# Entry 0's first 512 tokens two to a partition, in four rounds of four heads: what it does to the opening of a fused retention and MLP kernel

## The chip, the core and the metric

The kernel runs on one core of one Trainium2 chip. A core has a matrix engine (PE, with its weight loads shown apart as PEld), a vector engine (DVE), an activation engine (ACT), a general engine (POOL), a queue engine (SP) and 16 DMA engines. Work on PE reads SBUF and writes PSUM, which has eight banks; DVE and ACT bring results from PSUM to SBUF. The metric is the device time of one execution in microseconds, as the median of several runs.

## What is computed

```python
q, k, v: (8, 8, 576, 64)          # entries, heads, tokens, head size
scores = q @ k^T / 8              # within an entry and a head
gamma  = 1 - 2 ** (-5 - head)
ret    = (scores * gamma ** (i - j) for j <= i, else 0) @ v
x      = ret.transpose(0, 2, 1, 3).reshape(4608, 512)
h      = x @ w_in                 # 512 -> 2048
out    = (h / (1 + exp(-1.702 * h))) @ w_out      # 2048 -> 512
```

The kernel factors `gamma ** (i - j)` into a factor of the query's position (`gq`, applied to the output), one of the key's position (`vfac`, with the 1/8 in it, applied to the values or, for one block, elsewhere), and a mask of zeros and ones.

## The kernel before

**An order written out by hand.** The program records operations engine by engine in the order in which they are called (`R.op`), and each engine executes its own list strictly in that order. Waits follow from the named tiles (`r`, `w`) and PSUM banks (`ps`); PE doesn't wait for itself, except where `own=` names one of its earlier operations.

**The retention of one entry.** Entry 0 is handled in blocks of 128 tokens (four, and one of 64 tokens). For a block, PE turns queries and keys (`transposes`, L411, eight matmuls with the identity), ACT copies them to SBUF (`evac_t`, L418), PE forms the scores of the eight heads (`scores`, L431), DVE multiplies them by the mask into `sm` (`mask_s`, L441), PE multiplies by the values (`values`: L454), adds the part that comes from earlier blocks through the running state (L482), and extends the state with this block's keys and values (L467). ACT copies the state (`evac_z`, L505), and DVE multiplies the output by `gq` into `xT` (`evac_o`, L518), the transposed input of the MLP. In the block at 384 the factor `vfac` sits in the mask (`mask3`), so that its values can be used as they come; a scaled copy (`v3`) is made afterwards for the state. Blocks of the other entries are of 64 tokens and are handled in bursts (`burst`, `step`), which are mixed into the MLP.

**Loads.** Keys, queries and values of entry 0 are loaded by POOL, which casts them from f32 to bf16 on the way: one DMA for a block's eight heads, in pieces of one head's row of one token (`load`, L219). The first queries and values come by SP without a cast (`load_early`, L265). The weights follow in POOL's list (`load_w_in` L243, `load_w_out` L248), and two multiplications of values by `vfac` stand in it (`scale_v`, L390). Later loads wait on DVE's zeroing of unused halves (`constants_third`, `constants_shifted`).

**The MLP.** `hidden(c, f)` forms 128 of the 2048 hidden columns for 512 tokens (L732, four matmuls of 512 columns; ACT applies the activation, L737); `project` multiplies by `w_out` (L765). Chunk 0 is the first 512 tokens, so it needs all four blocks. Its first four hidden units are split by tokens (`hidden_part`, L843: 384 tokens, then 128) and put between the operations of the last block; `hidden(0, 4)` is the first ordinary unit. From there on PE runs hidden units, projections and bursts to the end. `fill` (L831) is matmuls on zeros whose result isn't used.

## Time and profile before

| | |
|---|---|
| runs | 299.64 us median (298.96, 299.64, 299.91) |
| the profiled execution | 298.93 us, span 297.1 us |
| PE | 291.1 us busy (98%), 3399 matmuls |
| DVE, ACT, POOL | 123.1, 125.9, 151.6 us busy |
| `project`, L765 | 544 matmuls, 122.0 us |
| `hidden`, L732 | 492 matmuls, 108.9 us |
| granted TensorE clock | 1.000 |

The span runs from the first to the last instruction; the time of an execution has some 1.8 us more around it. Times in the views below are microseconds from the span's start. A row of the timeline gives start, duration, engine, line, operation, tile written and tiles read, the part of the array that is used (rows*columns), the shape, the count, and in brackets the idle time before it with what ended it. A matmul's duration includes its way through the array, so that the rows of one engine overlap. In the chain of waits a row is start, duration, engine, tile, line and count.

### The profile page before, as it was taken

The numbers are of one execution on the slowest core, as the hardware profiler recorded it, in microseconds if no ns is written. First come the engines' busy times: TensorE is split into PE (matmuls) and PEld (weight loads), VectorE is DVE, ScalarE is ACT, GpSimd is POOL, SyncE is SP. The second block draws the span as 40 slices with busy tenths as digits, with TensorE's granted clock in tenths as the row PEclk, the third lists the DMA queues.
The fourth block names the chain that finished last, engine by engine and source line by source line (L and its number), as shares of the span: only waits on it lengthen the run. The fifth ranks groups of instructions, "written<-read, shape, count | busy, mean of one in ns | idle before, by whom it ended". The sixth has DMA issues, their size and how long they took to land.

```text
span 297.1 us, 7697 instructions
## 1 busy us (share of the span) xinstructions
PE 291.1 (98%) x3399; PEld 148.5 (50%) x3399; DVE 123.1 (41%) x221; ACT 125.9 (42%) x208; POOL 151.6 (51%) x205
## 2 busy tenths in 40 slices
PE   7799999999999999999999999999999999999996
PEld 3464455848544444544454445545454445444444
DVE  7769475454445435532615324245326504000012
ACT  6658426617256313540355045503660275026600
POOL 8975979989959887568984797000000000000000
PEclk9999999999999999999999999999999999999999
DMA  9999999999999999999999999904820200030012
GB/s 133 156 186 190 173 171 165 188 131 140 182 140 143 183 143 175 194 130 134 154 218 124 114 188 162 85 2 108 170 38 2 107 37 2 0 108 35 0 50 93
DMA packets 154850, 36.04 MB, mean 121 GB/s; under 512 B 145472, under 2 KB 150336, under 8 KB 154816
## 3 DMA queue, kind: packets, MB, share of 16 engines
q0 software_dynamic: 116304, 18.10, 94.1%
q1 hardware_dynamic: 38512, 17.44, 32.6%
q8 instruction: 27, 0.44, 0.6%
q14 instruction: 7, 0.06, 0.1%
HBM read 36.70 MB, written 9.44 MB: 155 GB/s over the span
## 4 chain that ended last, share of the span: by engine, by line
PE 94%; POOL 2%; DMA 2%; issue 0%; DVE 0%; POOLq 0%
PE psB L765 40%; PE psB L732 36%; PE psB L749 5%; PE psA L627 2%; DMA st_k<-in_k_dram 2%; PE psA L599 2%; PE psA L641 2%; PE psA L615 1%; PE psA L765 1%; PE psA L791 1%; PE psB L843 1%; PE psA L411 1%; POOL st_k L219 1%; POOL st_q L219 1%; POOL st_v L219 1%
## 5 line engine op out<-in xcount | busy, mean ns | idle before, releaser
L765 PE MATMUL psB<-w_out_sb,gT 128*128 128x512 bf16 x544 | 122.0, 380 | 0.0
L732 PE MATMUL psB<-xT,w_in_sb 128*128 128x512 bf16 x492 | 108.9, 379 | 0.0
L737 ACT ACTIVATE gT<-psB 128x512 bf16<-128x512 f32 x123 | 73.5, 597 | 38.4 <-PE psB L732 38.1
L765 PEld LDWEIGHTS psB<-w_out_sb,gT 128*128 128x128 bf16 x544 | 51.8, 98 | 60.2 <-DVE sm L696 0.3
L732 PEld LDWEIGHTS psB<-xT,w_in_sb 128*128 128x128 bf16 x492 | 47.5, 98 | 56.5
L685 DVE TENSOR_TENSOR xT<-psA,gq 128x768 bf16<-128x768 f32 x21 | 20.1, 958 | 115.3 <-PE psA L615 115.3
L232 POOL DMA_DIRECT2D st_k<-in_k_dram x70 | 52.5, 774 | 15.2 <-DMA st_k<-in_k_dram 10.9
L774 ACT ACTIVATE osb<-psB 128x512 f32<-128x512 f32 x31 | 18.5, 597 | 90.2 <-PE psB L765 86.8
L232 POOL DMA_DIRECT2D st_v<-in_v_dram x70 | 51.9, 767 | 5.7 <-DMA st_v<-in_v_dram 3.3
L219 POOL DMA_DIRECT2D st_q<-in_q_dram x39 | 34.8, 891 | 10.2 <-DMA st_q<-in_q_dram 7.6
L390 DVE TENSOR_TENSOR st_v<-st_v,vfac 128x512 bf16<-128x512 bf16 x36 | 23.3, 681 | 1.2 <-DMA st_v<-in_v_dram 1.2
L714 DVE TENSOR_TENSOR zacc<-zacc,psA 128x256 f32<-128x256 f32 x49 | 20.5, 419 | 6.9 <-PE psA L627 5.7
L696 DVE TENSOR_TENSOR sm<-psA,maskw 128x768 bf16<-128x768 f32 x21 | 19.9, 948 | 0.0
L749 PE MATMUL psB<-xT,w_in_sb 128*128 128x256 bf16 x128 | 15.0, 273 | 0.0
L777 DVE COPY osb<-psB 128x512 f32<-128x512 f32 x3 | 2.1, 692 | 29.7 <-PE psB L765 29.7
L749 PEld LDWEIGHTS psB<-xT,w_in_sb 128*128 128x128 bf16 x128 | 12.2, 98 | 1.7
L418 ACT ACTIVATE qk<-psA 128x1024 bf16<-128x1024 bf16 x8 | 8.2, 1022 | 9.8 <-PE psA L411 9.8
L599 PE MATMUL psA<-sm,st_v 64*64 64x64 bf16 x504 | 11.8, 195 | 0.3
L627 PE MATMUL psA<-st_v,st_k 64*64 64x64 bf16 x448 | 11.8, 199 | 0.0
L627 PEld LDWEIGHTS psA<-st_v,st_k 64*64 64x64 bf16 x448 | 7.5, 105 | 8.3 <-issue 7.8
L755 ACT ACTIVATE gT<-psB 128x512 bf16<-128x512 f32 x16 | 9.4, 599 | 5.0 <-PE psB L749 5.0
L615 PE MATMUL psA<-qk,zw 64*64 64x64 bf16 x448 | 11.1, 194 | 0.0
(103 smaller groups left out, 164.3 us busy)
## 6 DMA issues: line engine op xcount, KB each, us to landing
out_dram<-osb SPq DMA_DIRECT2D x35, 256.0 KB, 3.9
st_q<-in_q_dram POOLq DMA_DIRECT2D x31, 128.0 KB, 7.5
st_k<-in_k_dram POOLq DMA_DIRECT2D x57, 64.0 KB, 7.3
st_v<-in_v_dram POOLq DMA_DIRECT2D x57, 64.0 KB, 7.0
w_out_sb<-in_moe_w_out_dram POOLq DMA_DIRECT2D x4, 512.0 KB, 10.9
w_in_sb<-in_moe_w_in_dram POOLq DMA_DIRECT2D x3, 512.0 KB, 8.6
st_k<-in_k_dram POOLq DMA_DIRECT2D x4, 128.0 KB, 4.8
w_in_sb<-in_moe_w_in_dram POOLq DMA_DIRECT2D x2, 256.0 KB, 6.8
```

The source lines that it names most:

```text
L219: paced(R.op("POOL", lambda e, d=d, s=s: e.dma_start(d, s), w=[(nm, sl, c)], dma=(nm, sl, c), own=pace()))
L232: paced(R.op("POOL", lambda e: [e.dma_start(d, s) for d, s in parts], w=[(nm, sl, c)], dma=(nm, sl, c), parts=2, own=pace()))
L390: R.op(eng, lambda e: e.tensor_tensor(t, t, f, ALU.mult), r=[("vfac", min(b, 1))], w=[("v", sl, c)])
L627: i = e.matmul(psA[half(j), bank, off + 64 * t : off + 64 * t + 64], rows_of(st_k, m_in, g, u, h), rows_of(st_v, m_in, g, u, h), start=(t ...
L685: R.op("DVE", lambda e: e.tensor_tensor(xT[:, :, t0 : t0 + 192].rearrange("p (u j) n -> p u j n", u=2), psA[:, 2:4, 0:384].rearrange("p u ...
L696: R.op("DVE", lambda e: e.tensor_tensor(o, i, k, ALU.mult), r=["maskw"], w=[("sm", si(m))], ps=["S"])
L714: R.op("DVE", lambda e, to=to, src=src, was=was: e.tensor_tensor(to, was, src, ALU.add), r=[("zacc", (blk - 1) % 3)], w=[("zacc", blk)], p ...
L732: i = e.matmul(bank, w_in_sb[:, a, 128 * f : 128 * f + 128], xT[:, a, 512 * c : 512 * c + 512], start=(a == 0), stop=(a == 3))
L737: R.op("ACT", lambda e: e.activation(gT[c % 2][:, f, :], bank, AF.Gelu_apprx_sigmoid), w=[("gT", c % 2, f)], ps=[key])
L749: m = e.matmul(bank[:, 256 * i : 256 * i + 256], w_in_sb[:, a, 128 * (f + i) : 128 * (f + i) + 128], xT[:, a, a0 : a0 + 256], start=(a == ...
L765: i = e.matmul(bank, gT[c % 2][:, f, 128 * r : 128 * r + 128], w_out_sb[:, f, :], start=(f == 0), stop=(f == NF - 1))
L774: R.op("ACT", lambda e: e.activation(osb[m].ap(), bank, AF.Copy), w=[("osb", m)], ps=[key])
```

## The change

The first 512 tokens of entry 0 are now four rounds `n = 2 G + u`: `G` is the 256 tokens from `256 G`, `u` the four heads from `4 u`. Two neighbouring tokens lie in one partition, so a piece of a load is two rows of a head (`two_rows`), and a load has 4 heads x 128 pieces; the queries of rounds 2 and 3 come in one. Positions, factors and masks get a form for even and odd tokens. Within a round, tokens are treated as two blocks of 128 (`r`), held in the two halves of the partitions: scores and values use quarters of the array (64 rows by 64 columns), the state is extended after each block (`state_two`) and read by the next, and the matmuls of `values_two` are three groups, each of which waits for the one before it (`own=done`). Round 3 has `vfac` in its mask, as the block at 384 had, and now its keys are scaled into `k3` for the state, on POOL, where `v3` was a copy of the values. `scale_two(1)` is on DVE; rounds 2 and 3 have theirs on POOL behind the weights' first DMAs. The calls of the opening are put in a new order, the first four hidden units are split by 256 tokens and by heads, the zeroing of unused halves (`constants_third(0, 1)`) now stands behind all of them, and the last two extensions of the state follow unit 7, as one did before.

```diff
+        def load_two(n, nm, count=1):
+
+            src, dst = {"q": (q, st_q), "k": (k, st_k), "v": (v, st_v)}[nm]
+            s = two_rows(src, n, count)
+            d = dst[:, 0, n : n + count, :].rearrange("p c n -> p (c n)")
+            d = d.rearrange("p (h x) -> p h x", x=2 * DH)
+            paced(R.op("POOL", lambda e: e.dma_start(d, s),
+                       w=[(nm, 0, n + i) for i in range(count)], dma=(nm, 0, n), own=pace()))
+
+        def two_rows(src, n, count=1):
+            G, u = divmod(n, 2)
+            s = src[0, 4 * u : 4 * u + 4 * count, 256 * G : 256 * G + 256, :]
+            return s.rearrange("h (p s) d -> p h (s d)", s=2)
...
+            scale_two(0)
             for r in range(2):
                 rows = slice(64 * r, 64 * r + 64)
                 R.op("DVE", lambda e, rows=rows, r=r: e.tensor_single_scalar(
                     maskw[rows, :], rel[rows, 0:64], float(-64 * r), ALU.is_ge),
                     r=["rel"], w=["maskw"])
+                R.op("DVE", lambda e, rows=rows, r=r: e.tensor_single_scalar(
+                    mask[rows, 1, 0, :], rel[rows, 0:64], float(1 - 64 * r), ALU.is_ge),
+                    r=["rel"], w=["mask"])
+            R.op("DVE", lambda e: e.tensor_copy(
+                mask[:, 0, :, :], maskw.ap().unsqueeze(1).to_broadcast([P, 2, 64])),
+                r=["maskw"], w=["mask"])
+            R.op("DVE", lambda e: e.tensor_copy(mask[:, 1, 1, :], maskw.ap()),
+                 r=["maskw"], w=["mask"])
...
+        def scale_k3(eng):
+            f = vfac[0][:, 4:8, NC + 2 : NC + 4].unsqueeze(3).to_broadcast([P, 4, 2, DH])
+            o = k3.rearrange("p (h s d) -> p h s d", s=2, d=DH)
+            R.op(eng, lambda e: e.tensor_tensor(o, two(st_k, 3), f, ALU.mult),
+                 r=[("vfac", 0), ("k", 0, 3)], w=[k3_key])
+
+        def two(t, n):
+            return t[:, 0, n, :].rearrange("p (h s d) -> p h s d", s=2, d=DH)
+
+        def scale_two(n, eng="DVE"):
+            G, u = divmod(n, 2)
+            t = two(st_v, n)
+            i = early(1).rearrange("p (h s d) -> p h s d", s=2, d=DH) if n == 0 else t
+            f = vfac[0][:, 4 * u : 4 * u + 4, NC + 2 * G : NC + 2 * G + 2]
+            f = f.unsqueeze(3).to_broadcast([P, 4, 2, DH])
+            R.op(eng, lambda e: e.tensor_tensor(t, i, f, ALU.mult),
+                 r=[("vfac", 0)] + (early_keys(1) if n == 0 else []), w=[("v", 0, n)])
+
+        def transposes_two(n, at=None):
+            to, key = turned(at)
+
+            def fn(e):
+                for a, t in ((0, st_q), (1, st_k)):
+                    for s2 in range(2):
+                        for h in range(4):
+                            i = e.matmul(to[half(h % 2), a, 2 * s2 + h // 2, :],
+                                         two(t, n)[:, h, s2, :], ident.ap(),
+                                         is_transpose=True)
+                return i
+            R.op("PE", fn, r=["ident", ("q", 0, n), ("k", 0, n)], ps=[key])
+
+        def intra_two(n, pair):
+            at, keys = pairs[pair]
+            now = qk[n]
+
+            def fn(e):
+                for hp in range(2):
+                    for s2 in range(2):
+                        for r in range(2):
+                            for j in range(2):
+                                o = at[half(r), j, 2 * hp + s2, :]
+                                i = e.matmul(o.rearrange("p (s n) -> p s n", s=2),
+                                             now[half(j), 1, 2 * s2 + hp, half(r)],
+                                             now[half(j), 0, hp : 4 : 2, half(r)])
+                return i
+            R.op("PE", fn, r=[("qk", n, 0), ("qk", n, 1)], ps=keys)
+            m = mask.ap().rearrange("p k s n -> p (k s n)").unsqueeze(1).to_broadcast([P, 4, 256])
+            if n == 3:
+                m = mask3.rearrange("p (x y) -> p x y", y=256)
+            o = sm_all[n % 3].ap().rearrange("p (x y) -> p x y", y=256)
+            i = at.rearrange("p a (h k) n -> p (a h) (k n)", k=2)
+            R.op("DVE", lambda e: e.tensor_tensor(o, i, m, ALU.mult),
+                 r=mask3_keys if n == 3 else ["mask"], w=[("sm", n % 3)], ps=keys)
+
+        def state_two(n, r, out=True):
+            u = n % 2
+            ks = k3.rearrange("p (h s d) -> p h s d", s=2, d=DH) if n == 3 else two(st_k, n)
+
+            def fn(e):
+                for hp in range(2):
+                    for s2 in range(2):
+                        for j in range(2):
+                            h = 2 * hp + j
+                            i = e.matmul(psZ[half(j), 2 * u + hp, 0:64],
+                                         ks[half(r), h, s2, :],
+                                         two(st_v, n)[half(r), h, s2, :],
+                                         start=(n == 0 and r == 0 and hp == 0 and s2 == 0),
+                                         stop=False, skip_group_check=True)
+                return i
+            R.op("PE", fn, r=[k3_key if n == 3 else ("k", 0, n), ("v", 0, n)], ps=["Z"])
+            if out:
+                R.op("ACT", lambda e: e.activation(
+                    zq[r][:, 2 * u : 2 * u + 2, :], psZ[:, 2 * u : 2 * u + 2, 0:64], AF.Copy),
+                    w=[("zq", r, u)], ps=["Z"])
+
+        def values_two(n, o, inter_first=True):
+            po, key = o
+            G, u = divmod(n, 2)
+
+            def inter(e):
+                for r in range(2):
+                    if G == 0 and r == 0:
+                        continue
+                    for hp in range(2):
+                        for j in range(2):
+                            i = e.matmul(po[half(j), 2 * hp : 2 * hp + 2, half(r)],
+                                         zq[1 - r][half(j), 2 * u + hp, :],
+                                         qk[n][half(j), 0, hp : 4 : 2, half(r)],
+                                         start=(inter_first and hp == 0 and r == (G == 0)),
+                                         stop=not inter_first,
+                                         skip_group_check=True)
+                return i
+
+            def rows(e, r):
+                for hp in range(2):
+                    for s2 in range(2):
+                        for j in range(2):
+                            x = sm[n % 3][half(r), j, 2 * hp + s2, :]
+                            i = e.matmul(po[half(j), 2 * hp : 2 * hp + 2, half(r)],
+                                         two(st_v, n)[half(r), 2 * hp + j, s2, :],
+                                         x.rearrange("p (s n) -> p s n", s=2),
+                                         start=(not inter_first and r == hp == s2 == 0),
+                                         stop=(inter_first and s2 == 1), skip_group_check=True)
+                return i
+            parts = [(lambda e, r=r: rows(e, r), [("sm", n % 3), ("v", 0, n)]) for r in range(2)]
+            zs_of = [("zq", r, u) for r in range(1 + G)]
+            parts.insert(0 if inter_first else 2, (inter, [("qk", n, 0)] + zs_of))
+            done = None
+            for fn, reads in parts:
+                done = R.op("PE", fn, r=reads, ps=[key], own=done)
+            t0 = 256 * G
+            to = xT[:, 2 * u : 2 * u + 2, t0 : t0 + 256].rearrange("p h (n s) -> p h s n", s=2)
+            by = gq[:, 2 * u : 2 * u + 2, t0 : t0 + 256].rearrange("p h (n s) -> p h s n", s=2)
+            R.op("DVE", lambda e: e.tensor_tensor(
+                to, po.rearrange("p (h s) n -> p h s n", s=2), by, ALU.mult),
+                r=[("gq", 0), ("gq", 1)],
+                w=[("xU" if u else "xT", x) for x in range(4 * G, 4 * G + 4)], ps=[key])
...
-        load(0, 0, "k")
+        load_two(0, "k")
         constants_first()
-        load(0, 1, "qk")
-        load(0, 2, "qk")
-        load(0, 1, "v")
-        load(0, 2, "v")
-        load(0, 3, "qk")
+        load_two(1, "q")
+        load_two(1, "k")
+        load_two(1, "v")
+        load_two(2, "q", 2)
+        load_two(2, "k")
+        load_two(2, "v")
+        load_two(3, "k")
         load_w_in(0, 1)
+        load_two(3, "v")
         load_w_in(1, 2)
-        scale_v(1, "POOL")
-        scale_v(2, "POOL")
-        load(0, 3, "v")
         load_w_in(2, 4)
+        scale_two(2, "POOL")
+        scale_k3("POOL")
...
+        split = [(psW, "W"), (psU, "U"), (psA[:, 0, :], "S"), (psA[:, 2, :], "O")]
+        fourth = (psH[0].rearrange("p (h n) -> p h n", h=HP), ("H", 0))
+
+        def hidden_part(f, lo, hi, us=(0, 1)):
             bank, key = split[f]
 
             def fn(e):
-                for a in range(4):
-                    i = e.matmul(bank[:, lo:hi], w_in_sb[:, a, 128 * f : 128 * f + 128],
-                                 xT[:, a, lo:hi], start=(a == 0), stop=(a == 3))
-                return i
-            R.op("PE", fn, r=[("w_in", f // 2)] + [("xT", x) for x in range(lo // 64, hi // 64)],
-                 ps=[key])
-            if hi == 512:
+                for u in us:
+                    for a in (2 * u, 2 * u + 1):
+                        i = e.matmul(bank[:, lo:hi], w_in_sb[:, a, 128 * f : 128 * f + 128],
+                                     xT[:, a, lo:hi], start=(a == 0), stop=(a == 3),
+                                     skip_group_check=True)
+                return i
+            R.op("PE", fn, r=[("w_in", f // 2)] + [("xU" if u else "xT", x) for u in us
+                                                   for x in range(lo // 64, hi // 64)], ps=[key])
+            if hi == 512 and 1 in us:
                 R.op("ACT", lambda e: e.activation(gT[0][:, f, :], bank, AF.Gelu_apprx_sigmoid),
                      w=[("gT", 0, f)], ps=[key])
...
         fill(11)
         later_gq(0)
+        transposes_two(0)
+        evac_t(0)
+        state_two(0, 0)
         later_gq(1)
-        transposes(0)
-        evac_t(0)
+        fill(3)
+        intra_two(0, 0)
+        transposes_two(1, second)
+        evac_t(1, second)
+        state_two(0, 1)
+        scale_two(1)
         later_gq(2)
+        fill(2)
+        intra_two(1, 1)
+        values_two(0, third[0])
+        state_two(1, 0)
+        later_gq(3)
+        fill(2)
+        values_two(1, third[1])
+        state_two(1, 1)
+        transposes_two(2)
+        evac_t(2)
         constants_mask3()
-        fill(4)
-        transposes(1, second)
-        evac_t(1, second)
-        intra(0)
-        fill(4)
-        intra(1, 1)
-        transposes(2)
-        evac_t(2)
-        values(0, third[0])
-        evac_z(0)
-        evac_o(0, third[0])
-        later_gq(3)
-        fill(2, second)
-        intra(2)
-        values(1, third[1])
-        evac_z(1)
-        evac_o(1, third[1])
-        fill(1)
-        transposes(3)
+        fill(2)
+        intra_two(2, 0)
+        state_two(2, 0)
+        transposes_two(3)
         evac_t(3)
-        values(2, third[0])
-        evac_z(2)
-        evac_o(2, third[0])
-        fill(1)
         gelu_table()
-        intra(3)
+        hidden_part(1, 0, 256)
+        intra_two(3, 1)
+        values_two(2, third[0])
+        hidden_part(0, 0, 256)
+        state_two(3, 0)
+        hidden_part(2, 0, 256)
+        values_two(3, fourth, False)
+        for f in range(3):
+            hidden_part(f, 256, 512, (0,))
+        hidden_part(3, 0, 256)
+        hidden_part(3, 256, 512, (0,))
+        for f in range(4):
+            hidden_part(f, 256, 512, (1,))
         constants_third(0, 1)
...
-        hidden(0, 4, (psA[:, 0, :], "S"))
-        for f in range(5, NF):
+        hidden(0, 4, wide_banks[2])
+        hidden(0, 5, wide_banks[1])
+        for f in range(6, NF):
             hidden(0, f, next_bank())
             if f == 7:
-                values(3, third[0], "state")
-                evac_z(3)
+                state_two(2, 1, False)
+                state_two(3, 1, False)
+                evac_z()
```

## What I predict

> **What bounds the kernel now.** I read the page's slices first, then the busy time by stretches, then the chain in order of time, then the waits, and last single PE rows.
>
> ```profile
> PE   7799999999999999999999999999999999999996
> PEclk9999999999999999999999999999999999999999
> ...
> 10.00:20.00 10.00, 8.48 (x138) 5.38 (x138) 6.76 (x11) 5.07 (x8) 8.84 (x12) 1.00 1.74 169
> 20.00:30.00 10.00, 9.97 (x66) 4.89 (x65) 9.33 (x22) 7.32 (x15) 6.67 (x9) 1.00 1.21 193
> ```
>
> The first number after each stretch's length is PE's busy time: 8.48 of 10 us up to 20 us, 9.97 afterwards. From about 21 us PE never waits again, so whatever happens later on another engine is hidden as long as that stays so, and the change is worth exactly what it moves the start of the first ordinary hidden unit (`hidden(0, 4)`, whose weight load starts at 21.57), plus matmuls added or removed after it.
>
> ```profile
> 8.74 6.04 DMA st_k<-in_k_dram
> 14.91 0.61 PE psA L411 x8
> 15.52 0.34 PE psA L454 x8
> 15.99 0.36 PE psA L482 x8
> 16.37 0.70 DVE xT L518
> 17.12 2.12 PE psB L843 x12
> ...
> PE psA L411 <- DMA st_k<-in_k_dram: 1.3, 1, 1.3
> ```
>
> The chain says that the opening is set by the issue of ten loads on POOL and the landing of the last keys at 14.78 (issue 8.74, 6.0 to landing); PE waited 1.3 us for them. From there to 21.57 are 6.7 us, nearly all PE work. So an earlier landing is worth something only if PE, ACT and DVE have finished the earlier rounds by then, and if the 6.7 us stay 6.7.
>
> **Prices of PE work**, from these rows:
>
> ```profile
> 14.91 0.38 PE L411 MATMUL psA<-ident,st_q 128*128 128x128 bf16 x4 [1.32 <-DMA st_k<-in_k_dram]
> 15.13 0.39 PE L411 MATMUL psA<-ident,st_k 128*128 128x128 bf16 x4
> 15.45 0.41 PE L454 MATMUL psA<-sm,st_v 128*64 128x128 bf16 x8
> 15.70 0.29 PE L467 MATMUL psA<-st_v,st_k 128*64 128x64 bf16 x8
> 15.92 0.41 PE L482 MATMUL psA<-qk,zq 64*64 64x128 bf16 x8
> 16.26 0.39 PE L831 MATMUL psB<-idle 128*128 128x512 bf16 x1
> ...
> 65.22 0.27 PE L615 MATMUL psA<-qk,zw 64*64 64x64 bf16 x12
> 65.57 0.26 PE L599 MATMUL psA<-sm,st_v 64*64 64x64 bf16 x8
> ```
>
> - One matmul of 128 columns runs 0.22, of which it holds the array 54 ns (four whole-array ones in 0.38). Eight that alternate between two halves take 0.41, so 27 ns each; 64 columns, half. Groups over all four quadrants: L641 has 24 of 64 columns in 0.40, (0.40 - 0.20) / 23 = 9 ns each; for 128 columns I take 54 / 4 = 13.5.
> - Tail: the next engine starts 0.18 + 0.05 after the last slot of a group.
> - Change of array shape: the state group begins at 15.70 and its eight slots of 13.5 ns end at 15.81; the next shape starts at 15.92. 0.12 each.
> - Self-wait (`own=`: PE waits for its own last matmul): the twelve inter matmuls end at 65.49, the next group starts at 65.57. Tail 0.18 + 0.08 = 0.26 each.
>
> With these and the rows of ACT (copy of turned tiles 1.02) and DVE (mask 1.23, output 0.69) the kernel before comes out at 21.56 from its transposes at 6.40 and the landing; the trace has 21.57.
>
> [...]
>
> **The change, part by part.**
>
> *Loads.* A load for eight heads by 128 tokens (1024 pieces, 0.88 to 0.94 on POOL) becomes one of four heads by 256 tokens (512 pieces). The nearest row with 512 is the 64-row load of entry 0 at 0.70; I take 0.75. POOL then issues first keys 1.25, three iotas, queries/keys/values of round 1 from 2.6, the double query load, keys 2 and values 2, keys 3 at about 7.2 (before: 8.74). At the 4.5 us to landing that loads in this stretch show, keys 1 land at 7.8, values 1 at 8.6, round 2 by 10.5, keys 3 by 11.7 to 13.2. First keys: 6.25 now, 0.2 less issue, 6.05; bounds 5.87 (the eleven fills end) and 6.40 (no gain). The extra iota and `vfac` columns cost about 0.2 and lie before that landing. None of the other landings is reached by PE before it has come (next part), so they cost and give nothing; 2 us is the cover.
>
> *DVE.* Masks now take six small operations, about 1.2 us (rows: 64x64 at 0.19, 128x128 at 0.22), but the 1.4 of the fourth round's masks moves behind; DVE is free at 7.35, its first scores come at 8.33. `scale_two(1)` (0.69) moves from POOL to DVE behind the first mask. Outputs written with a step of two: between 0.69 and double; on this ladder even 1.04 changes nothing.
>
> *ACT.* Six state copies of half size (row: 0.38 for 256; by the 1.02 for 1024, 0.27) in place of three; hidden except where named.
>
> *PE, laid out in the new order.* Transposes 0 are 16 half-array matmuls, 0.43 plus 0.10 for the slow first ones (before: 0.53 for four): 6.05 to 6.58. ACT copy 6.81 to 7.83. Scores 0 (16 over four quadrants, 0.22) at 7.88. Transposes 1 8.22 to 8.65, copy 8.88 to 9.90 (ACT carries `later_gq(1)` until 8.82). Scores 1 9.95 to 10.17. Values 0 = inter 0.11, self-wait 0.26, rows 0.22, self-wait 0.26, rows 0.22 = 1.07, to 11.24; state 0.10; two fills with their change of shape 0.56, to 11.90; values 1 12.02 to 13.09; state 0.10; transposes 2, which stand behind all this in PE's queue though their loads landed at 10.5, 13.31 to 13.74. Copy 13.97 to 14.99. Scores 2 15.04 to 15.26, state 0.10, transposes 3 15.48 to 15.91 (keys 3 landed long ago), copy 16.14 to 17.16. Scores 3 at 17.21. Before: 16.64.
>
> From there PE works without a pause: scores 0.22; values 2 (inter 0.22, twice rows 0.22, two self-waits) 1.18; change + hidden part 0.55; change + state 0.22; change + hidden part 0.55; change + values 3 1.30; change 0.12; three upper parts 0.66, last part 0.43 + 0.22, lower parts 0.86. Sum 6.31, so `hidden(0, 4)` at 23.52. The same stretch before took 21.57 - 16.64 = 4.93. DVE keeps up: mask 1 ends 11.63 (rows of values 1 need it at 12.39), mask 2 16.72 (17.91), mask 3 18.89 (20.05), last output 22.15 (needed 22.66).
>
> *Behind it.* The deferred states are 16 matmuls in place of 8: 0.11. The DVE memsets that release the load of the last 64 tokens move behind the last output, so that load is issued at about 23 instead of 18.98. It now lands at 32.1 behind 13 us of queued weights and is read at 34.23 (then 36.2); a queue that is as full delivers it about as before. Nothing.
>
> **Sum:** 23.52 - 21.56 + 0.11 = +2.1 us. Span 297.1 becomes 299.2; the profiled execution's own 298.93 becomes 301.0. That execution was 0.7 under the median of the runs, so for the median 299.64 + 2.1 = **301.7**. What makes it: eight self-waits, all on the path, 8 x 0.26 = 2.0. Without them the ladder ends at 21.51, level with before.
>
> **Bounds of what the trace does not show.** Scores over four quadrants: 0.22 taken, 0.43 if only two overlap: +0.8. Half-array transposes: 0.43 by L454, 0.86 if they don't overlap: +1.7. Row groups: 0.22 by L482, 0.11 if they spread over four quadrants: -1.2. First landing: -0.1 to +0.35. Self-wait: 0 to 0.26: -2.0 to 0. The forecast's own range, with one of these off, 300.5 to 303.4.
>
> **Rivals.**
> 1. *Arrival is the bound, and the rest follows it* (faster). If keys 3 land at 12.2 and the 6.7 us behind them stay, `hidden(0, 4)` starts at 19.0: -2.5, **297.1**. For it: the chain and the 1.3 us wait. Against it: PE's queue reaches transposes 3 at 15.48 by the ladder. It decides where rounds 0 to 2 are through PE by 12.4, which needs self-waits and changes of shape near nothing. 0.15.
> 2. *Self-waits are covered* (level). If the array keeps other work in flight so that they cost nothing, 21.51 + 0.11: **299.7**. For it: half of them fall into rounds 0 and 1, where PE used to run fills. Against: the gap at 65.49 to 65.57, in each later burst alike. 0.12.
> 3. *A later landing takes over* (slower still). If POOL needs 0.9 per load as before and the weights, now issued between the values, slow the queue, keys 2 come after 13.3; at 15 PE, standing at transposes 2, loses 1.7: **303.4**. Against: 2.8 us of cover. 0.08.
> 4. *The change doesn't do what it says for the loads*: issue and landing as before. Then only the first landing counts, +0.35: **302.1**, inside the forecast.
>
> **How the numbers follow.** Forecast with rival 4: 0.65. A measurement of this kernel can tell about 0.3%, 0.9 us. Slower by more: 0.65 + 0.08 = 0.73, less a little for the forecast's lower edge, 0.72. Level: 0.11. Faster: 0.17. The range leaves out rival 1 and the far end of rival 3: 298.9 to 303.6.
>
> **What would show it.** In the profile after: PE gaps of about 0.26 between the two row groups of each round and around the inter group; transposes 2 at about 13.3 with no DMA wait; keys 3 landed before 13.5; scores 3 near 17.2; the first L732-type unit near 23.5; PE full from there. Wrong if PE waits for a load after 8 us, if transposes 3 start before 14.9, if the groups follow one another without gaps, or if PE shows gaps after 24 us.

## The result, and the profile after

The changed kernel takes **301.91 us** (median of six runs, 301.39 to 302.89). The kernel before, run beside it six times, takes 300.0 (298.96 to 300.22). The ratio is **1.0074**, 95% interval 1.0051 to 1.0097. The profiled execution took 301.64 us with a span of 299.9 (before 298.93 and 297.1). Of all executions in this document one, of more_self_waits, was in a slower state (311.06 us, clock 0.966); it is left out of the medians and ratios.

The same views as before, in the same order. PE's slices on the page:

```profile
PE   8789998999999999999999999999999999999996
```

Two stretches (length, then PE, PEld, DVE, ACT and POOL busy with their counts, the granted clock, DMA share and GB/s):

```profile
10.00:20.00 10.00, 7.98 (x175) 5.17 (x174) 7.99 (x8) 5.58 (x10) 6.63 (x8) 1.00 1.40 186
20.00:30.00 10.00, 9.82 (x88) 5.61 (x89) 7.84 (x19) 6.07 (x12) 5.81 (x7) 1.00 1.32 192
```

PE is busy for 7.98 us between 10 and 20 us, where it was 8.48, with more and smaller matmuls. From 20 to 30 us it is 9.82 in place of 9.97, but what is missing there stands before 24 us, in the opening, which is now longer:

```profile
20.00:24.00 4.00, 3.82 (x47) 3.00 (x48) 2.22 (x6) 0.98 (x3) 1.20 (x2) 1.00 1.24 206
24.00:30.00 6.00, 6.00 (x43) 2.61 (x42) 5.62 (x14) 5.09 (x11) 4.61 (x6) 1.00 1.37 182
```

The chain of waits in the opening:

```profile
9.49 0.45 PE psB L450 x16
9.94 0.02 issue
9.96 1.24 DVE sm L460
11.20 0.05 issue
11.25 0.60 PE psB L927 x2
11.85 0.25 PE psB L494 x4
12.10 0.04 issue
12.14 0.43 PE psB L507 x8
12.57 0.04 issue
12.62 0.41 PE psB L507 x8
13.03 0.12 PE psA L472 x8
```

No DMA is left in the chain, which begins with the eleven fills: the loads went off the path. What took their place are copies by ACT, a mask by DVE and PE's own ends. The two row groups of round 1 (L507) start at 12.14 and 12.62, 0.48 apart, and eight such matmuls hold the array for 0.22 (8 x 27 ns, the forecast's estimate from L454); the other 0.26 is the wait of PE for itself. All four rounds show such a pair (18.32 less 17.85 in round 2). But the two self-waits of round 0 are not on the chain: from scores 1 it runs over DVE, which makes mask 1 until 11.20, while PE does the values of round 0 and is done 0.17 us earlier; the two fills wait for that mask, whose bank they write. So six of the eight self-waits lie on the chain, two in each of the rounds 1 to 3. Single PE rows say the same of the loads:

```profile
13.08 0.41 PE L434 MATMUL psA<-ident,st_q 128*64 128x128 bf16 x8
...
14.84 0.42 PE L450 MATMUL psA<-qk 64*64 64x128 bf16 x16 [0.58 <-ACT qk L548]
...
17.06 0.42 PE L450 MATMUL psB<-qk 64*64 64x128 bf16 x16 [0.57 <-ACT qk L548]
```

Transposes 2 have no bracket: PE reached them without a pause, since their keys had landed (12.2). Scores 2 and 3 wait for ACT's copy, as laid out.

The weight loads (PEld) behind the opening:

```profile
23.36 2.37 PEld L825 LDWEIGHTS psB<-xT,w_in_sb 128*128 128x128 bf16 x12
26.11 0.55 PEld L825 LDWEIGHTS psB<-xT,w_in_sb 128*128 128x128 bf16 x4 [0.38 <-ACT gT L831]
27.08 0.20 PEld L472 LDWEIGHTS psA<-st_v,st_k 64*64 64x64 bf16 x8 [0.42 <-issue]
```

`hidden(0, 4)` starts at 23.36 instead of 21.57: +1.79. From there to the end are 299.9 - 23.36 = 276.54 us, where it was 297.1 - 21.57 = 275.53: +1.01. The two make the 2.8 us of span. The view of PE's waits from 24 us on (waiting operation, what it waited for, total, times, longest) was empty for the kernel before, and now has

```profile
PE psB L859 <- issue: 2.2, 14, 0.2
PE psB L825 <- issue: 1.0, 6, 0.2
PE psA L859 <- DVE zacc L807: 0.4, 1, 0.4
PE psB L859 <- ACT osb L868: 0.2, 1, 0.2
PE psB L825 <- ACT gT L831: 0.2, 1, 0.2
```

The 22 waits of 0.16 us each in four of these rows go with matmul records that this trace lacks (522 and 483 matmuls of the two lines for 544 and 496 weight loads). In state3_before_hidden below, which has the same operations from 24 us on and all 544 and 496 records, the view has the L807 row alone. That one is a wait, 0.36 us at 48.1 us. DVE is late there, after copies of regrouped weights; in the kernel before,

```profile
39.75 0.42 DVE L337 COPY gT<-w_in_sb 64x1024 bf16<-64x1024 bf16 x1
40.21 0.54 DVE L338 COPY w_in_sb<-w_in_sb 64x1024 bf16<-64x1024 bf16 x1
40.79 0.71 DVE L339 COPY w_in_sb<-gT 64x1024 bf16<-64x1024 bf16 x1
```

and in the changed one

```profile
41.79 0.73 DVE L359 COPY gT<-w_in_sb 64x1024 bf16<-64x1024 bf16 x1
42.56 0.71 DVE L360 COPY w_in_sb<-w_in_sb 64x1024 bf16<-64x1024 bf16 x1
43.30 0.71 DVE L361 COPY w_in_sb<-gT 64x1024 bf16<-64x1024 bf16 x1
```

The same three copies take 2.15 instead of 1.67, and the next three, right before the late sum, 1.49 instead of 1.26; POOL issues loads beside them in both kernels, and what slows them is not settled.

### The profile page after: what moved, and what is told of

The parts are those of the page before. It is cut to its first block, busy times and chain, and to the rows that moved or that the text cites. A ratio compares the mean times of both kernels' runs of the same rounds, so it can differ in the third digit from the quotient of the medians.

```text
span 299.9 us, 7920 instructions
## 1 busy us (share of the span) xinstructions
PE 288.7 (96%) x3487; PEld 150.2 (50%) x3524; DVE 125.1 (42%) x224; ACT 126.6 (42%) x211; POOL 151.0 (50%) x205
## 4 chain that ended last, share of the span: by engine, by line
PE 92%; DVE 3%; ACT 2%; issue 2%
PE psB L859 37%; PE psB L825 36%; PE psB L843 5%; PE psA L720 2%; PE psB L927 2%; PE psA L692 2%; ACT qk L548 2%; PE psA L734 1%; PE psA L708 1%; PE psA L885 1%; PE psA L941 1%; PE psA L859 1%; PE psA L434 1%; PE psB L507 1%; DVE w_in_sb L361 0%
## 5 line engine op out<-in xcount | busy, mean ns | idle before, releaser
L859 PE MATMUL psB<-w_out_sb,gT 128*128 128x512 bf16 x522 | 117.7, 379 | 2.7 <-issue 2.2
L825 PE MATMUL psB<-xT,w_in_sb 128*128 128x512 bf16 x483 | 107.7, 379 | 1.4 <-issue 1.0
L219 POOL DMA_DIRECT2D st_q<-in_q_dram x36 | 32.5, 903 | 8.7 <-DMA st_q<-in_q_dram 4.2
L807 DVE TENSOR_TENSOR zacc<-zacc,psA 128x256 f32<-128x256 f32 x49 | 20.5, 418 | 7.0 <-PE psA L720 5.8
L843 PEld LDWEIGHTS psB<-xT,w_in_sb 128*128 128x128 bf16 x128 | 12.2, 98 | 1.7
```

The costliest lines, as they stand in the source:

```text
L219: paced(R.op("POOL", lambda e, d=d, s=s: e.dma_start(d, s), w=[(nm, sl, c)], dma=(nm, sl, c), own=pace()))
L807: R.op("DVE", lambda e, to=to, src=src, was=was: e.tensor_tensor(to, was, src, ALU.add), r=[("zacc", (blk - 1) % 3)], w=[("zacc", blk)], p ...
L825: i = e.matmul(bank, w_in_sb[:, a, 128 * f : 128 * f + 128], xT[:, a, 512 * c : 512 * c + 512], start=(a == 0), stop=(a == 3))
L843: m = e.matmul(bank[:, 256 * i : 256 * i + 256], w_in_sb[:, a, 128 * (f + i) : 128 * (f + i) + 128], xT[:, a, a0 : a0 + 256], start=(a == ...
L859: i = e.matmul(bank, gT[c % 2][:, f, 128 * r : 128 * r + 128], w_out_sb[:, f, :], start=(f == 0), stop=(f == NF - 1))
```

## The experiments

The opening is compared from the start of scores 0, because that start moves from run to run (7.17 to 8.13 us): the first keys land 4.0 to 4.9 us after their issue, and the eleven fills end between 5.1 and 6.1 us. "Rest" is the span less the start of the first ordinary hidden unit.

| kernel | transposes 2 | scores 3 | first unit | rest | median us | before beside it | ratio (95%) |
|---|---|---|---|---|---|---|---|
| changed | 5.71 | 9.69 | 15.99 | 276.54 | 301.91 | 300.0 | 1.0074 (1.0051 to 1.0097) |
| more_self_waits | 7.31 | | 20.58 | 276.58 | 306.98 | 299.05 | 1.0246 (1.0170 to 1.0321) |
| no_fill_round1 | 5.83 | | 17.71 | 276.64 | 304.0, one run | 299.05 | |
| state3_before_hidden | | 9.68 | 15.66 | 276.57 | 301.89, one run | 299.05 | |
| weights_before_keys2 | 6.75 | | 17.97 | 277.13 | 304.93, one run | 299.05 | |
| covered_waits | 6.51 | 11.12 | 16.45 | 276.3 | 301.89, one run | 299.88 | |
| late_regroup | | | 15.98 | 275.99 | 301.94, one run | 299.88 | |
| bank_order | | | 16.08 | 276.41 | 301.44, one run | 299.88 | |
| all_three | 5.02 | 9.66 | 15.01 | 276.02 | 300.08 | 299.88 | 1.0007 (0.9986 to 1.0028) |
| scores3_ahead | 4.94 | 8.96 | 14.33 | 275.69 | 299.99 | 299.43 | 1.0017 (1.0003 to 1.0031) |
| fill_moved | 5.79 | 9.77 | 16.08 | 277.07 | 302.73, one run | 299.43 | |

### More self-waits

The groups of `values_two` are halved, so that each round has five waits of PE for itself in place of two.

```diff
-            parts = [(lambda e, r=r: rows(e, r), [("sm", n % 3), ("v", 0, n)]) for r in range(2)]
+            parts = [(lambda e, r=r, hp=hp: rows(e, r, (hp,)), [("sm", n % 3), ("v", 0, n)])
+                     for r in range(2) for hp in range(2)]
...
```

> Each of the three groups of a round's values is split in two, each half waiting for the one before: five self-waits a round in place of two, twelve more in all, no other work. Theory (a self-wait on PE's path costs 0.26): round 0 hides 0.18 behind the mask of round 1, the rest is on the path, 12 x 0.26 - 0.18 = +2.9; the first ordinary hidden unit starts near 26.6 in place of 23.7, the span grows to about 302.8. Rival (self-waits are covered by work in flight, and what costs is the arrival or the smaller matmuls): first unit at 23.7, span 299.9.

The chain shows one wait after another:

```profile
13.35 0.26 PE psB L494 x2
13.61 0.04 issue
13.65 0.32 PE psB L507 x4
13.97 0.04 issue
14.02 0.32 PE psB L507 x4
```

Four matmuls, which by the same estimate hold the array for 0.11, recur every 0.37: 0.26 for the wait. The three waits added in round 0 say the same. From scores 1 to the fills it is 2.37 us (10.14 to 12.51) in place of 1.76 (9.49 to 11.25), 0.61 more, and the 0.17 for which PE waited for mask 1 is used up as well: 0.78 for three. So the price of a self-wait is shown, and equals the 0.26 of the forecast. (Transposes 2 move from 5.71 to 7.31, 1.60 for six waits, but from 14.5 us on the clock is at one half, ahead of their start at 15.35.) The first unit came at 28.62, where 26.6 was expected. Of the 5.3 us by which the span grew, 0.67 is the later start of scores 0 and, at 0.26 each less 0.17, some 2.9 are the twelve waits; the rest, some 1.7, goes with another thing: the granted clock is 0.50 for 6.8 us.

### The fills between rounds 0 and 1

```diff
         later_gq(3)
-        fill(2)
         values_two(1, third[1])
```

> The two idle matmuls between the values of round 0 and round 1 are left out (their result is used nowhere). In the changed kernel they wait for the mask of round 1, whose bank they write, and cost two changes of array shape. Theory (PE's own queue sets the path): the inter matmuls of round 1 then wait for the state copy at 11.47 instead, 0.26 earlier than 11.78, and transposes 2 start at 12.8 (keys 2 landed at 12.2): first unit at 23.4. Rival (loads set the path): no change. A second rival: without the fills PE's clock falls, transposes and scores of rounds 2 and 3 take twice as long, first unit later than 24.5.

The inter group of round 1 came 0.28 earlier (4.13 after scores 0, for 4.41), and then the clock fell to one half and the time rose by some 2 us. So the fills hold PE for 0.28 us. Whether their absence is what let the clock fall, a second kernel was to tell: it leaves the same two fills out, and puts two more ahead of scores 2 and two ahead of scores 3.

> The changed kernel without the two fill matmuls between the values of rounds 0 and 1; these two stand ahead of scores 2 instead, and two more between the first hidden part and scores 3. Theory (the clock fell in no_fill_round1 because PE's work in that stretch got too thin, and the fills cost what they hold PE): inter of round 1 at 4.13 after scores 0 (4.41 in the changed kernel), transposes 2 at 5.4 (5.71), the first unit near 15.7 (15.99), if the clock stays at 1.0. Rival: one stretch without fills is enough for the clock to fall, wherever the others stand; then the first unit is at 17.0 or later and the time near 303 to 304.

The clock stayed at 1.00 throughout. Keys 1 landed late here (PE waited 0.21 for them, and scores 1 came at 2.38 after scores 0 for 2.12); from scores 1 to the inter group of round 1 it was 2.03 for 2.29, the same gain. The late keys took it back: transposes 2 at 5.79 and the first unit at 16.08, where 5.4 and 15.7 were expected. But the two kernels are alike up to transposes 2, at 13.5 us, and the clock had fallen before that. Half-microsecond stretches of no_fill_round1 (columns as above):

```profile
12.50:13.00 0.50, 0.44 (x12) 0.28 (x9) 0.00 (x0) 0.50 (x1) 0.50 (x1) 0.84 1.45 195
13.00:13.50 0.50, 0.50 (x16) 0.50 (x12) 0.02 (x1) 0.02 (x1) 0.50 (x2) 0.50 1.55 183
...
19.50:20.00 0.50, 0.35 (x9) 0.14 (x7) 0.50 (x1) 0.49 (x2) 0.00 (x0) 0.84 1.21 203
```

and of fill_moved:

```profile
12.50:13.00 0.50, 0.39 (x8) 0.28 (x8) 0.04 (x1) 0.42 (x1) 0.50 (x1) 1.00 1.52 195
13.00:13.50 0.50, 0.44 (x17) 0.42 (x16) 0.00 (x0) 0.30 (x1) 0.50 (x2) 1.00 1.49 173
```

The kernel whose clock held was even the less busy one from 5 to 13 us (6.10 us of PE work for 6.68). So my theory, that the work in that stretch had got too thin, is not shown, and neither is its rival: with identical code the clock fell in one run and not in the other, and each of the two kernels ran once. The time of fill_moved, 302.73, comes from elsewhere: its rest is 0.5 longer, with a wait of 1.0 us at the place where the changed kernel waits 0.4 for DVE (L807).

### A change of array shape

```diff
         values_two(2, third[0])
-        hidden_part(0, 0, 256)
         state_two(3, 0)
+        hidden_part(0, 0, 256)
```

> The state of round 3 stands directly behind the values of round 2 instead of between two hidden parts: the same matmuls, two changes of array shape less on the path. Theory (0.12 each): first unit 0.24 earlier, 23.45. Rival (changes of shape cost nothing): 23.7.

The first unit came 0.33 earlier. The quarter-array state group now follows quarter-array values, and two changes of shape are gone. That would be 0.16 each, but the trace has the state's eight matmuls among the last of the second row group (18.93 to 19.02), so the 0.10 for which they hold the array no longer shows either. Less that, it is some 0.12 each, as in the forecast. The time of the one run, 301.89, can't show 0.3.

### The loads' cover

```diff
         load_two(2, "q", 2)
+        load_w_in(0, 1)
+        load_w_in(1, 2)
         load_two(2, "k")
         load_two(2, "v")
         load_two(3, "k")
-        load_w_in(0, 1)
         load_two(3, "v")
-        load_w_in(1, 2)
```

> The first two loads of w_in are issued ahead of keys 2, values 2, keys 3 and values 3, which so come 1.6 later in POOL's list. In the changed kernel keys 2 land at 12.2 and transposes 2 start at 13.08. Theory (0.9 of slack): keys 2 land at 13.8 to 14.2, transposes 2 right behind, 0.8 to 1.2 later than now, and the first unit with them, 24.5 to 24.9. Rival (the landing sets the path already): the whole 1.6 to 2.0, first unit 25.3 to 25.7.

With the first weights ahead of keys 2, PE waits at transposes 2:

```profile
13.47 0.29 PE L472 MATMUL psA<-st_v,st_k 64*64 64x64 bf16 x8
14.75 0.41 PE L434 MATMUL psA<-ident,st_q 128*64 128x128 bf16 x8 [0.99 <-DMA st_k<-in_k_dram]
```

This is the mechanism of rival 3, made on purpose: transposes 2 at 6.75 for 5.71. The changed kernel stands 0.9 us clear of it (landing 12.2, use 13.08), where the forecast had 2.8. The loads came later than expected (keys 2 at 14.6 for 13.8 to 14.2), and behind them the clock was at 0.50 from 16.8 to 20.2. So the first unit is 1.98 later in all, at 25.97, outside the 24.5 to 24.9 of the theory.

### Covering the self-waits

`values_two` is taken apart, so that PE has other work between its groups: the groups of rounds 0 to 2 are interleaved with a state extension, with the next round's inter group, with transposes 2 and with scores 3. The computation is the same.

```diff
-        values_two(0, third[0])
+        v0, v1 = values_steps(0, third[0]), values_steps(1, third[1])
+        v0[0]()
         state_two(1, 0)
+        v0[1]()
+        v0[2]()
+        v0[3]()
...
+        v1[0]()
+        v1[1]()
+        fill(3)
         transposes_two(2)
         evac_t(2)
+        v1[2]()
+        state_two(1, 1)
+        v1[3]()
...
```

> The same matmuls and the same eight self-waits, in another order, so that other work of PE stands in the waits: state 1 behind the inter group of round 0, transposes 2 (with three idle matmuls ahead) between the two row groups of round 1, scores 3 between those of round 2; the inter group and first row group of round 2 move into the time in which PE waited for the keys of round 3 to be copied; the masks of round 3 are made earlier on DVE. Theory (self-waits and the place of transposes 2 in PE's queue set the path): counted from the start of scores 0, transposes 2 start when keys 2 have landed, 4.9 in place of 5.7, scores 3 at 8.9 in place of 9.7, and the first ordinary hidden unit at 14.1 in place of 16.0. Rival (the smaller matmuls themselves cost the time, or the landing): 15.5 to 16.0.

Undecided: values 1 landed late in this run (DVE waited 0.76 us for them, PE 0.64 behind it), and the clock was at 0.50 from 11.75 to 15.2, so the ladder can't be read (first unit at 16.45, where 14.1 was expected).

### What stands behind the opening

Two edits, one for each wait that the profile after shows. The regrouping of a weight on DVE moves behind the burst of the next unit:

```diff
-             7: [(scale_v, 5), (turn, 6)], 8: [(scale_v, 6), (regroup, 3)], 9: [(burst, None, 0, "ACT")],
+             7: [(scale_v, 5), (turn, 6)], 8: [(scale_v, 6)], 9: [(burst, None, 0, "ACT"), (regroup, 3)],
```

> The last exchange of rows in w_in (three copies on DVE) moves from ahead of the first burst's sums to behind them; nothing else. In the changed kernel these copies ran at 0.42 to 0.71 each, and PE waited 0.36 at 48 us for the sums. Theory: that wait goes, and from the first ordinary hidden unit to the end it takes 276.2 in place of 276.5. Rival (the wait comes from the loads of entry 1): 276.5.

The wait near 48 us is gone and the rest is 275.99 for 276.54: 0.55 less, of which the wait itself was 0.36. The other edit puts units 4 and 5 into each other's banks:

```diff
-        hidden(0, 4, wide_banks[2])
-        hidden(0, 5, wide_banks[1])
+        hidden(0, 4, wide_banks[1])
+        hidden(0, 5, wide_banks[2])
```

> The first two ordinary hidden units exchange their PSUM banks, so that unit 7 reuses the bank of unit 4 and not that of unit 5. In the changed kernel PE's weight loads sat idle for 0.38 ahead of unit 7, waiting for ACT to empty that bank. Theory: the wait goes, first unit to end 276.2 in place of 276.5. Rival (ACT is behind by four activations anyway, and unit 8 waits instead): 276.5.

Rest 276.41, only 0.13 less, where I expected 0.34; and even this can't be put down to the banks, since the wait for DVE at 48 us isn't in this trace either, and all_three below, with both edits, has no less than late_regroup alone. The wait of 0.38 at 26.11 is gone from PEld:

```profile
23.29 3.23 PEld L825 LDWEIGHTS psB<-xT,w_in_sb 128*128 128x128 bf16 x16
26.94 0.20 PEld L472 LDWEIGHTS psA<-st_v,st_k 64*64 64x64 bf16 x8 [0.42 <-issue]
```

but from the first unit to the deferred states it is 3.65 us, and with the wait it was 3.72. The last four weight loads run in 0.55 behind the wait and at some 0.8 without it: the weight loads were ahead of the matmuls, and the wait used that up. The idle time of PEld was not one of PE here.

### All together

`covered_waits`, `late_regroup` and `bank_order` in one kernel.

> The order of covered_waits, the late exchange of rows and the exchanged banks together. If the three gains add up: 1.9 + 0.3 + 0.38 = 2.6 under the changed kernel's 301.9, so 299.3, ratio to the kernel before 0.998 (level, or just faster). If the self-waits are not what costs: 301.2, ratio 1.004.

300.08 us, ratio **1.0007** (0.9986 to 1.0028): level with before. That lies between the two cases put down for it: 0.8 above the 299.3 of three gains that add up, 1.1 below the 301.2 of self-waits that cost nothing. Transposes 2 came at 5.02 (4.9 expected), and the rest is 276.02. Scores 3 gained next to nothing, though (9.66):

```profile
15.02 0.61 PE L949 MATMUL psB<-xT,w_in_sb 128*128 128x256 bf16 x4
15.56 0.24 PE L498 MATMUL psA<-qk,zq 64*64 64x128 bf16 x2
16.26 0.35 PE L498 MATMUL psA<-qk,zq 64*64 64x128 bf16 x6 [0.46 <-issue]
16.77 0.27 PE L511 MATMUL psA<-sm,st_v 64*64 64x128 bf16 x3 [0.15 <-PE psA L498]
16.83 0.24 PE L450 MATMUL psB<-qk 64*64 64x128 bf16 x1
```

PE paused for 0.46 us within the inter group of round 2, and nothing in the trace released it; the self-wait of the row group that I had put ahead of scores 3 (L450) came on top. The order alone doesn't make the pause: covered_waits has the same order there, and its eight matmuls follow without one (17.73, lasting 0.41). The last kernel puts scores 3 directly behind the inter group, and covers round 3 as well.

```diff
...
         v2[0]()
-        v2[1]()
         intra_two(3, 1)
+        v2[1]()
+        state_two(3, 0)
         v2[2]()
         v2[3]()
-        state_two(3, 0)
         hidden_part(0, 0, 256)
         hidden_part(2, 0, 256)
-        values_two(3, fourth, False)
-        for f in range(3):
+        v3[0]()
+        v3[1]()
+        hidden_part(0, 256, 512, (0,))
+        v3[2]()
+        v3[3]()
+        for f in range(1, 3):
             hidden_part(f, 256, 512, (0,))
```

> The kernel of all_three with the scores of round 3 straight behind the inter group of round 2, the first row group of round 2 behind them, a state extension between its two row groups, and one hidden part between the last row group and the inter group of round 3. Theory (the self-waits and PE's order are what is left of the opening): scores 3 at 9.1 after scores 0 (9.66 in all_three), the first ordinary unit at 14.5 after them (15.01), the rest 276.0 as in all_three, so 0.5 us less: a span near 297.7, a median near 299.5, 0.998 of the kernel before. Rival: the pause of 0.46 us that stood inside the inter group of round 2 stands there again and moves scores 3 with it; then they come at 9.5 or later and the median is again about 300.0.

The ladder came out as expected: scores 3 at 8.96, the first unit at 14.33, the rest 275.69.

```profile
16.19 0.41 PE L498 MATMUL psA<-qk,zq 64*64 64x128 bf16 x8
16.84 0.42 PE L450 MATMUL psB<-qk 64*64 64x128 bf16 x16 [0.23 <-ACT qk L556]
17.08 0.39 PE L511 MATMUL psA<-sm,st_v 64*64 64x128 bf16 x8
17.31 0.29 PE L472 MATMUL psA<-st_v,gT 64*64 64x64 bf16 x8
17.53 0.41 PE L511 MATMUL psA<-sm,st_v 64*64 64x128 bf16 x8
```

The row groups at 17.08 and 17.53 have the state group between them. They are still 0.45 apart: the wait has not gone, the state group stands in it. The pause in the inter group is not there, and that is most of the gain at scores 3: they start 0.65 after the inter group, as in covered_waits (0.64), and 1.27 in all_three. So the new order is not shown to move their start. The time did not follow: 299.99 us, ratio 1.0017 (1.0003 to 1.0031), no better than all_three, although scores 0 to the end is 1.0 us less in the profile. In this execution scores 0 itself came at 7.88, 0.71 later than in all_three, mainly because the eleven fills ended later (transposes 0 start at 6.00, for 5.41 in all_three). The keys had landed by then, 4.5 us after their issue at 1.25; the chain of this trace begins with the fills, which take 4.87 us from 1.19 on, for 4.18 in all_three. That start eats most of the gain in the profiled execution; whether it also holds the median was not tried. No version here beats the kernel before.

## Why the prediction was right

**The mechanism.** The forecast was +2.1 us, to 301.7; measured were 301.91, and +1.9 between the medians run side by side. It gave eight self-waits on the path as the whole of it, "8 x 0.26 = 2.0", and "level with before" without them. The price held: 0.26 by the rows of more_self_waits. The count did not: six lie on the chain, 6 x 0.26 = 1.56, since the two of round 0 pass while DVE makes mask 1. The forecast's own numbers had this: its fills start at 11.34, its mask 1 ends at 11.63, but it asked only when the values need that mask, not the fills.

With other groups between the waits the first unit comes 0.98 (all_three, from 15.99 to 15.01) and 1.66 us (scores3_ahead, to 14.33) sooner, with the new loads, tiles and shapes all kept. Both have the state of round 3 moved as in state3_before_hidden, which alone gave 0.33. So at most 1.33 of the 1.66 is from the waits, about five times 0.26, and one self-wait is left on the chain of scores3_ahead. That fits, but it is not isolated: these kernels also move transposes 2, the masks of round 3 and fills, and a kernel without the waits was not run. Nor do the waits explain the whole: the first unit of scores3_ahead, at 22.21, is still 0.64 behind the 21.57 of the kernel before, where the forecast had 21.51 without them. all_three is level with before only with the two edits behind the opening.

**The ladder**, point by point, in us from the start of scores 0:

| step | forecast | measured |
|---|---|---|
| scores 0, from the span's start | 7.88 | 7.37 |
| transposes 2 | 5.43 | 5.71 |
| scores 3 | 9.33 | 9.69 |
| `hidden(0, 4)` | 15.64 | 15.99 |
| from scores 3 to `hidden(0, 4)` | 6.31 | 6.30 |

- *First keys.* Forecast 6.05, bounds 5.87 to 6.40; they were used at 5.62, below the lower bound, since they landed 4.2 us after their issue at 1.25 and the eleven fills ended at 5.69, not 5.87. A gain of 0.43, by luck of this execution: with the same first load and fills transposes 0 start between 5.41 and 6.29 in the other ten kernels, in six of them at 5.99 or 6.00. In the profiled execution the early start made up for the 0.35 that the ladder behind it came out longer. (The bound of -0.1 put down for it is -0.18 by the forecast's own 5.87.)
- *Up to transposes 2* 0.28 more than forecast: 0.17 of it is a wait of the two fills between the rounds for mask 1 (`[0.17 <-DVE sm L460]`), which reads the bank that they write. I had not named that wait.
- *From scores 3 on* the sum of 6.31 held within 0.01, self-waits, half-array groups and shape changes together. The far ends of the bounds are excluded: the work behind scores 2 starts 0.25 after them (14.84 to 15.09; 0.22 forecast, bound 0.43), and ACT starts on transposes 2 0.68 after these began (13.08 to 13.76; 0.66 by the forecast of 0.43, 1.09 by the bound of 0.86).
- *Loads.* Issue 0.76 to 0.79 (0.75 forecast). Keys 1 at 7.65 and values 1 at 8.6 as forecast (7.8, 8.6); round 2 was late, its keys at 12.2 instead of 10.5; keys 3 at 13.65, just past the 11.7 to 13.2. The cover was 0.9 us, not 2 (or 2.8, as rival 3 has it), and it was enough. Rival 3 lost by that 0.9, and weights_before_keys2 shows it as real.
- *Masks.* `constants_mask3` took 2.45 us where I had 1.4, while POOL multiplied beside it; mask 2 still ended at 17.29, ahead of its use at 17.85. The operations take 2.02 to 2.45 in the six kernels where they overlap POOL's multiplications by 0.7 us or more (2.12 in all_three, 2.13 in scores3_ahead), and 1.40 to 1.53 in the five where the overlap is 0.54 at most (1.40 in covered_waits, with 0.54, and in fill_moved, where POOL is done first; 1.42 before). Why they are slower beside POOL no run here shows.

**Where it was wrong.** "Behind it. [...] Nothing." The profile was said to be wrong "if PE shows gaps after 24 us", and it does: the rest grew by 1.01 where 0.11 was forecast. 0.55 is the regroup on DVE (late_regroup), 0.13 at most the order of banks (bank_order), 0.11 the forecast states; some 0.2 is unaccounted for. Each figure is from one execution, and the wait for DVE alone is 0.3 to 1.0 us from run to run where nothing behind the opening was changed. So the span grew by 1.79 + 1.01 = 2.8 where the forecast was 1.96 + 0.11 = 2.07. That the median still came within 0.2 of the forecast is in part luck, and has to do with the executions that were profiled: the one of before was 1.07 under the median beside it, the one of after 0.27 under its own, so the medians are only 1.9 apart.

**The rivals.** 1, arrival as the bound: fell for the changed kernel, PE waits for no load after 8 us, and transposes 3 started at 15.31 with their keys there since 13.65. 2, covered self-waits: fell in rounds 1 to 3, whose six are on the chain; in round 0 it holds, though because of the mask. The order of all_three makes more of it true. 4: fell, the loads are as short as the diff says.

## What to carry to other kernels

Before taking a load off the path, lay out what PE does between the landing and the end, and price each wait of PE for itself (0.26 us here): six of them make 1.56 us here. Only those on the chain count, so look at each for another engine that is busy longer. Another group of matmuls can stand in such a wait (the state group between the row groups of round 2 in scores3_ahead, which start 0.45 us apart with it and 0.47 without it in the changed kernel), so order by groups, not by whole blocks. A stretch called hidden should be searched for the engine that is nearly late there, as DVE was at 48 us.

## What the hardware showed that was not expected

**The clock.** In four kernels of this study the granted clock of TensorE went from 1.00 to 0.50 in the opening, though behind its first fill PE was idle for at most 1.05 us at a time; sixteen score matmuls then took 0.64 for 0.42. Taking the half-microsecond stretches' means, it was at one half for 3.4 us (weights_before_keys2, covered_waits) or 6.8 us (no_fill_round1, 12.84 to 19.66; more_self_waits, 14.5 to 21.33): once or twice the same length. What sets that length, and what makes the clock fall, no run here shows: it fell with no idle gap of PE above 1.05 us, and of two kernels alike up to transposes 2, at 13.5 us, no_fill_round1 had the fall at 12.84 and fill_moved none.

**The first fills.** The eleven fills at the start follow one another every 0.43 us, and from some point on every 0.22, the pace of the hidden units behind the opening, with 1.00 in the clock column of the changed kernel throughout. Where the pace changes differs from run to run: in scores3_ahead all eleven go at 0.43 (the last two start at 5.01 and 5.44), in all_three the last two are 0.21 apart (4.78 and 4.99). This moves the start of the opening by up to 0.6 us.

**Weight loads run ahead.** In the changed kernel those of `hidden(0, 4)` start 0.33 us before its matmuls (23.36, 23.69). A bank wait of 0.38 on PEld cost 0.07 us of time (3.72 us for 3.65 from the first unit to the deferred states).
